# A fused attention and gated feed-forward block on one core: the four compute queues in a new order, and thirty operations on another engine

## The chip, the cores and the metric

The kernel runs on one core of a Trainium2 chip. The metric is the device time of one execution in microseconds. A core has four compute engines: TensorE (PE, matmuls; PEld are its weight loads), VectorE (DVE), ScalarE (ACT) and GpSimd (POOL). A fifth queue, SyncE (SP), issues nearly all transfers here. Each engine runs its own instructions strictly in order, and waits on semaphores for the others.

## The reference

One transformer block on x of 2048 rows by 448 columns, bf16. First a layer norm and a linear attention with 16 heads of 28:

```
qkv = layernorm(x) @ wqkv
pq = q @ w_phi ; pk = k @ w_phi                    (per head, 28x28)
phi_q = [softmax(pq), softmax(-pq)] ; phi_k likewise
kv = sum_s phi_k * v ; z = sum_s phi_k
o = (phi_q @ kv) / (phi_q @ z + 1e-6)
h = x + o @ wo
```

Then a second layer norm and a gated feed-forward with 1792 inner columns:

```
g = layernorm(h) @ w_gate ; u = layernorm(h) @ w_up
out = h + (sigmoid(g) * u) @ w_down
```

## The kernel before

The rows are cut into 16 tiles of 128, written t = 0 to 15, and into four chunks of 512 columns once they are transposed. Weights stay in SBUF. A weight or an activation has 448 inner columns, which are held as four blocks of 128 that overlap in part; matmuls use 64 rows each and run as pairs, one on the low half of the array and one on the high half. A pair of phases, named a and b (`pva4`, `pvb4`), covers one product: eight matmuls, then six. The b phase writes the banks of the a phase with the halves changed over, so it waits until the a phase has drained unless something stands between.

Every piece of work has a name, and a table `ORDER` (line 243) lists for each of the five queues the names in the order in which that engine executes them. A small graph (class `Graph`) derives the waits from what each piece reads and writes. Where a piece may run on several engines, the queue in which its name stands decides. So the order of the work, and the engine for many pieces, is written out by hand in `ORDER`, and nothing else sets it.

The names, with t a tile, c a chunk, k a block, f one of 14 blocks of inner columns of the feed-forward:

- `x`, `ld_k`, `ld_v`, `ld_q`, `ld_wo..`, `ld_wg`, `ld_wu`, `ld_wd` (SP): loads. `PACE` holds `ld_wg0` back until `pvb15` and `ld_wg1` until `kva14` have run.
- `warm` (PE, L532): matmuls on zeros, in the gaps of the head.
- `bst`, `agg` (DVE, L553, L554): row statistics of x. `pow1`, `nm1`, `nb1` (L562, L561, L569): factor, negated mean, offset. `xn` (L578 to L584): the normalised tile; on GpSimd it needs `nm1`. `xT`: its transpose, on TensorE for t below 4 (L546, copied from PSUM by `xT0e` and so on, L539), by a DMA transpose from SP for the others (L591).
- `wT`, `wTe`, `w2m0`, `w2e0`: the key weight is transposed (L607), copied, multiplied by w_phi (L620) and copied again, so that keys and their feature map are one matmul. `w2m1`, `w2e1`: the same for queries.
- `pp`, `vv` (t below 4) and `pv` (the others): feature map and values of a tile. `v1` (L539): the values copied out of PSUM. `ek` (ACT, L679, L680): the two exponentials. `ss`, `rs` (DVE, L683, L689): their sums and reciprocals. `phi` (L693): the product, on VectorE or GpSimd. `kva`, `kvb` (PE): phi times v, all tiles summed in two PSUM banks that `seed` (L717) starts.
- `pqa`, `pqb`, `eq` (L731): the queries' features, by chunk. `qs`: sums of the first two tiles. `kvzA` to `kvzD`: the finished kv, masked by heads.
- `num` (PE), then on VectorE `rsm`, `qq`, `b`, `c`, `rden` (L808 to L816) and `o` (L820): attention of a tile. `oT`: its transpose. `woa`, `wob`, `wof`: output projection; `h` (L840, L846): the residual. `sq`, `ve`, `nm`, `pow2`, `hn`, `hT`: second norm and transpose (for t of 0 and 1 `bs2` and `ag2` take the statistics from PSUM).
- `ga`, `gb` (PE, L334): gate and up of a column block f, for two tiles (names 0_f and 2_f) or a chunk of four (4_f, 8_f, 12_f). `sig` (ACT, L920): sigmoid. `uc` (ACT, L925): up copied out of PSUM, for 0_2 to 2_13. `hh` (L926): the product; on VectorE or GpSimd where `uc` exists.
- `dn`, `dp`, `dm`, `dl` (PE): down projection. `fin` (L960), `out`: last sum and store.

`num` uses PSUM banks 6 and 7 for nearly every tile, so `num6` waits until `c5` has read them. The banks of ff f are 4 and 5 for even f, 0 and 1 for odd f; a bank is free when `sig` and `uc` or `hh` have read it.

Of the kernel before, what the change touches and what calls it, by code (L numbers as in the profile page):

```python
# [18 lines left out]
class Graph:  # L19
# [109 lines left out]
    def emit(self, nc):  # L129
# [120 lines left out]
    ),  # L250
    "act": (
# [11 lines left out]
    ),  # L263
# [22 lines left out]
    ),  # L286
    "dve": (
# [15 lines left out]
    ),  # L303
    "pool": (
# [6 lines left out]
    ),  # L311
}
PACE = {"ld_wg0": "pvb15", "ld_wg1": "kva14"}
# [718 lines left out]
```

## Time and profile before

| | us |
|---|---|
| median of three runs (202.85 to 203.33) | 202.95 |
| the profiled execution | 203.83 |
| its span, first to last instruction | 202.0 |
| PE busy | 195.5 |
| DVE busy | 130.6 |
| ACT busy | 99.0 |
| POOL busy | 65.0 |

The span is the part that the profile shows in detail; the rest of the profiled execution's time lies around it. Times in the rows are microseconds from the start of the span; a row of the timeline gives the start, the length, the engine, the line, the operation and the tile, and in brackets the idle time before it and what ended it. Matmuls are pipelined, so the rows of two matmuls overlap, and the work of one is better read from start to start. The granted TensorE clock is full throughout.

### The profile page before, as it was taken

What the parts mean: (1) busy time and instruction counts of PE and PEld (TensorE: products, weight loads), DVE (VectorE), ACT (ScalarE), POOL (GpSimd) and SP (SyncE); (2) the same over time, 40 slices, a digit from 0 to 9 for tenths busy, and PEclk for the clock granted to TensorE, in tenths of its full rate; (3) what the DMA queues carried; (4) which work ended last, traced back from release to release, by engine and by line L of the source; (5) the groups of instructions that cost most, each with busy time, mean ns of one, the idle gap of its engine ahead of it and who ended that gap; (6) DMA issues with size and microseconds to landing.
All of it is one profiled execution on the core that took longest, in us unless ns stands there. A gap on an engine that the chain in (4) does not pass through costs nothing.

```text
span 202.0 us, 5879 instructions
## 1 busy us (share of the span) xinstructions
PE 195.5 (97%) x2500; PEld 114.7 (57%) x2500; DVE 130.6 (65%) x317; ACT 99.0 (49%) x212; POOL 65.0 (32%) x104
## 2 busy tenths in 40 slices
PE   7799999999989999999999999999999999999995
PEld 2745555575558887786444444555555555554443
DVE  6899999979899981646767967436432422272224
ACT  3758998798795866444333342324422212222220
POOL 5499986932425865540042020001400000000000
PEclk9999999999999999999999999999999999999999
DMA  6957542657996271221006511030212000004002
GB/s 165 303 119 126 80 83 58 178 191 242 301 190 150 55 83 27 28 55 26 5 0 81 123 29 26 3 76 23 55 49 52 2 0 3 0 3 136 0 0 91
DMA packets 32866, 16.25 MB, mean 80 GB/s; under 512 B 25096, under 2 KB 31944, under 8 KB 32840
## 3 DMA queue, kind: packets, MB, share of 16 engines
q1 hardware_dynamic: 32336, 15.86, 35.6%
q8 instruction: 19, 0.31, 0.7%
q10 hardware_dynamic: 504, 0.03, 0.2%
q14 instruction: 7, 0.06, 0.1%
HBM read 8.34 MB, written 1.84 MB: 50 GB/s over the span
## 4 chain that ended last, share of the span: by engine, by line
PE 90%; DVE 4%; DMA 2%; SPq 1%; ACT 1%; issue 1%
PE psum L334 81%; PE psum L953 5%; DMA wk_sb<-in_A_wqkv_dram 2%; DVE ss L683 2%; DVE xn_pad L581 1%; PE psum L620 1%; PE psum L532 1%; SPq L435 1%; PE psum L895 1%; PE psum L546 1%; DVE rs L689 0%; DVE b_sb L811 0%; PE psum L607 0%; DVE c_sb L814 0%; ACT v L539 0%
## 5 line engine op out<-in xcount | busy, mean ns | idle before, releaser
L334 PE MATMUL psum<-xnT,wg_sb 64*128 64x512 bf16 (+1 forms) x490 | 93.3, 334 | 0.1
L334 PE MATMUL psum<-xnT,wu_sb 64*128 64x512 bf16 (+1 forms) x490 | 92.9, 334 | 0.0
L920 ACT ACTIVATE sg_sb<-psum 128x512 bf16<-128x512 f32 (+1 forms) x70 | 35.2, 514 | 75.3 <-PE psum L334 74.8
L926 DVE TENSOR_TENSOR hhT<-sg_sb,psum 128x512 bf16<-128x512 bf16 (+1 forms) x44 | 28.9, 672 | 46.8 <-ACT sg_sb L920 46.5
L334 PEld LDWEIGHTS psum<-xnT,wg_sb 64*128 64x128 bf16 x490 | 44.4, 94 | 21.1 <-DVE hhT L926 2.3
L334 PEld LDWEIGHTS psum<-xnT,wu_sb 64*128 64x128 bf16 x490 | 44.4, 94 | 12.5
L334 PE MATMUL psum<-wd_sb,hhT 64*128 64x448 bf16 x336 | 37.1, 349 | 0.0
L334 PEld LDWEIGHTS psum<-wd_sb,hhT 64*128 64x128 bf16 x336 | 17.9, 94 | 14.0 <-DVE x_sb L846 0.5
L334 PE MATMUL psum<-Wk,xnT 64*128 64x448 bf16 x112 | 22.0, 351 | 0.1
L334 PE MATMUL psum<-wv_sb,xnT 64*128 64x448 bf16 x112 | 22.1, 351 | 0.0
L693 POOL TENSOR_TENSOR phi<-hhT,rs 128x896 bf16<-128x896 bf16 x10 | 17.7, 1775 | 2.8 <-DVE rs L689 2.6
L683 DVE TENSOR_REDUCE ss<-hhT 128x32 f32<-128x896 bf16 x16 | 16.7, 1057 | 0.2
L855 POOL TENSOR_SCALAR ve<-ssq 128x1 f32<-128x1 f32 x10 | 2.0, 202 | 45.6 <-ACT junk L852 45.3
L731 ACT ACTIVATE eq<-psum 120x1024 bf16<-120x1024 f32 x16 | 15.7, 1027 | 0.9 <-PE psum L334 0.6
L820 POOL TENSOR_TENSOR o_pad<-c_sb,rden 128x448 bf16<-128x448 bf16 x11 | 10.2, 935 | 15.7 <-DVE rden L816 13.6
L334 PE MATMUL psum<-xnT,Wq 64*120 64x512 bf16 x112 | 14.8, 384 | 0.1
L925 ACT CAST xn_pad<-psum 128x256 bf16<-128x256 f32 x26 | 9.8, 380 | 6.9 <-PE psum L334 6.4
L960 DVE SCALAR_TENSOR_TENSOR x_sb<-psum,x_sb 128x448 bf16<-128x448 f32 (+2 forms) x17 | 9.4, 592 | 3.8 <-PE psum L334 1.9
L334 PE MATMUL psum<-wo_o,oT 64*128 64x448 bf16 x49 | 11.5, 349 | 0.0
L334 PE MATMUL psum<-wo_e,oT 64*128 64x448 bf16 x49 | 11.5, 349 | 0.0
L679 ACT ACTIVATE hhT<-psum 128x448 bf16<-128x448 f32 x16 | 8.8, 547 | 5.4 <-PE psum L334 5.2
L953 PE MATMUL psum<-wd_sb,hhT 128*128 128x448 bf16 (+2 forms) x70 | 11.2, 316 | 0.0
(113 smaller groups left out, 256.9 us busy)
## 6 DMA issues: line engine op xcount, KB each, us to landing
out_dram<-x_sb SPq DMA_DIRECT2D x15, 112.0 KB, 1.8
x_sb<-in_A_x_dram SPq DMA_DIRECT2D x7, 224.0 KB, 4.9
wd_sb<-in_B_w_down_dram SPq DMA_DIRECT2D x7, 224.0 KB, 5.4
wg_sb<-in_B_w_gate_dram SPq DMA_DIRECT2D x3, 448.0 KB, 5.2
wu_sb<-in_B_w_up_dram SPq DMA_DIRECT2D x3, 448.0 KB, 4.5
wv_sb<-in_A_wqkv_dram SPq DMA_DIRECT2D x2, 224.0 KB, 5.4
wk_sb<-in_A_wqkv_dram SPq DMA_DIRECT2D x2, 196.0 KB, 3.9
wo_e<-in_A_wo_dram SPq DMA_DIRECT2D x1, 336.0 KB, 3.2
```

Of the source, the lines that this page charges most:

```text
L334: p = e.matmul(o, lhsT=w, rhs=r, start=st, stop=sp, tile_position=(row, 0))
L435: return op(eng, name, lambda e: e.dma_start(dst, src), r=r, w=w, dma="in" if eng == "sp" else "ain", nring=(48 if eng == "sp" else 8) if ...
L679: e.activation(ek[:, s, :, 0, :], src, ACT.Exp)
L683: op("dve", "ss%d" % t, lambda e: e.tensor_reduce(ss[:, s, :].rearrange("p (b h) -> p b h", h=2), eks.rearrange("p b (d h) -> p b h d", h= ...
L693: return e.tensor_tensor(phi[:, sp, :, :, :].rearrange("p b a n -> p (b a) n")[:, :, 0:56].rearrange("p b (d h) -> p b d h", h=2), eks.rea ...
L731: op("act", "eq%d_%d%s" % (c, i, "pm"[sg]), lambda e, sg=sg: e.activation(eq[c][:, sg, 2 * i:2 * i + 2, :].rearrange("p g n -> p (g n)"), ...
L820: return e.tensor_tensor(o_pad[:, t % NO, off:off + D].rearrange("p (h d) -> p h d", h=H), c_sb[:, t % NS, :, 0:DH], rden[:, t % NS, :][:, ...
L920: op("act", "sig" + nm, lambda e: e.activation(sg_sb[:, k, 0:N], bk(bg)[:, 0:N], ACT.Sigmoid), r=[B(bg)], w=[("sg", k)])
L925: op("act", "uc" + nm, lambda e: e.copy(up, bk(bu)[:, 0:N]), r=[B(bu)], w=[ub])
L926: op(("pool", "dve") if nm in UCOPY else "dve", "hh" + nm, lambda e: e.tensor_tensor(hhT[(t0 // 4) % NHH][:, ff, ns], sg_sb[:, k, 0:N], up ...
L953: p = e.matmul(bk(b)[:, lo:hi], lhsT=hb[:, ff, TS(t)], rhs=wd_sb[:, ff, lo:hi], start=ff == 0, stop=ff == FT - 1)
L960: op("dve", "fin%d%s" % (t, nm), lambda e: e.scalar_tensor_tensor(out=h_sb[:, t, lo:hi], in0=bk(b)[:, lo:hi], scalar=1.0, in1=h_sb[:, t, l ...
```

## The change

Four of the five queues of `ORDER` are rewritten; SP's stays as it is, and no operation is added or removed. The new table is one text line shorter, so the same code has line numbers lower by one afterwards.

Thirty operations change engine:

- From DVE to ACT: `xT0e`, `xT2e`, `v1_13`. From ACT to DVE: `wTe3`, `v1_11`.
- From POOL to ACT: `nm1_4`, `nm1_12`.
- From DVE to POOL: `phi8`, `hh0_2`, `hh0_5`, `hh0_6`, `hh0_9`, `hh2_1`, `hh2_2`, `hn5`, `hn6`, `ve2`, `ve6`.
- From POOL to DVE: `phi9`, `hh0_3`, `hh0_4`, `hh0_8`, `hh2_0`, `hh2_3`, `hn3`, `o9`, `nm2`, `nm3`, `nm7`, `ve5`.

Within the queues many neighbours change places. The core of the difference by queue:

```diff
 "act":
-wTe0 wTe1 xT1e wTe3 w2e0_0 w2e0_2 w2e0_3 ek0 ek1 v1_0 v1_1 ek2 w2e1_1 nm1_8 v1_2 ek3 v1_3 w2e1_3 v1_4 ek4
+wTe1 wTe0 xT1e xT0e w2e0_0 w2e0_2 w2e0_3 nm1_4 xT2e ek0 ek1 v1_0 par v1_1 ek2 w2e1_1 v1_2 v1_3 ek3 w2e1_3 nm1_8 ek4 v1_4
...
-ek6 v1_6 ek7 v1_7 v1_8 ek8 eq0_0m ek9 v1_9 ek10 v1_10 ek11 v1_11 ek12 v1_12 ek13 eq0_0p par ek14 ek15 v1_14 v1_15
+ek6 v1_6 ek7 v1_7 nm1_12 ek8 v1_8 eq0_0m ek9 v1_9 ek10 v1_10 ek11 ek12 v1_12 ek13 v1_13 eq0_0p ek14 ek15 v1_15 v1_14
...
-uc0_2 sq3 sig0_5 uc0_5 uc0_4 sig0_4 sq2 uc0_7
+uc0_2 sq2 uc0_5 sig0_5 uc0_4 sig0_4 sq3 uc0_7
...
-sig0_8 uc0_8 sq5 uc0_11 sig0_11 sig0_10 uc0_10 uc0_13 sig0_12 sig0_13 uc0_12 sq7 uc2_0 sig2_0 sig2_1 uc2_1 sq6
+uc0_8 sig0_8 uc0_11 sig0_11 uc0_10 sig0_10 sq5 sq6 sig0_13 sig0_12 uc0_13 uc0_12 sq7 uc2_0 sig2_0 sig2_1 uc2_1
 "pe":
-warm0 wT0 wT1 xT1 warm1 warm2 warm3 wT2 wT3 w2m0_0 xT0 warm4 warm5 w2m0_2 w2m0_1 w2m0_3 warm6 warm7 warm8
-ppa0 warm9 ppb0 vva0 xT2 xT3 vvb0 ppa2 ppb2 vva2 w2m1_1 vvb2 seed w2m1_0 w2m1_3 kva0 pva4 kvb0 pvb4 pva5
+warm0 wT1 wT0 warm1 xT1 warm2 warm3 xT0 w2m0_0 wT2 wT3 warm4 warm5 w2m0_2 w2m0_1 w2m0_3 warm6 warm7 warm8
+ppa0 xT2 ppb0 xT3 warm9 vva0 vvb0 ppa2 seed ppb2 vva2 w2m1_1 vvb2 kvb0 w2m1_0 w2m1_3 pva4 kva0 kvb1 pvb4 pva5
...
-pva11 kvb6 pvb11 pva12 kva6 kvb7 pvb12 kva7 kvb8 pva13 kva8 pvb13 pva14 kvb10 pvb14 pva15 kva10 kvb9 pvb15 kva9
+kvb6 pva11 kva6 pvb11 pva12 kvb7 pvb12 pva13 kva7 kvb8 pvb13 kva8 pva14 kva10 pvb14 pva15 kvb10 kva9 pvb15 kvb9
...
-kvb15 kva14 qs pqa1_1 wwo num0
+kvb15 kva14 pqa1_1 qs wwo num0
...
-ga0_10 gb0_11 gb0_10 wob6 num10 ga0_13 ga0_12 gb0_13 gb0_12 dn0_0 dn0_4 ga2_1 ga2_0
+ga0_10 gb0_11 gb0_10 num10 wob6 ga0_13 ga0_12 gb0_13 gb0_12 dn0_0 dn0_4 ga2_0 ga2_1
 "dve":
-bst2 xn0 bst3 wTe2 agg2 agg3 xT0e bst4 w2e0_1 bst5 bst7 agg4 agg5 bst6 agg7 agg6 bst11 bst8 bst10 xT2e xT3e
+xn0 bst3 bst2 agg3 wTe2 wTe3 agg2 bst5 w2e0_1 bst4 agg5 bst6 agg4 bst10 agg6 bst7 bst11 xT3e
...
-phi5 ss8 rs7 rs8 xn13 xn14 ss9 ss10 rs10 phi8 ss11 rs9 rs11 ss12 v1_13 rs12 phi11
+phi5 ss8 rs7 xn13 ss9 rs8 xn14 ss10 v1_11 rs10 ss11 rs9 rs11 ss12 phi9 rs12 phi11
...
-rsm4 qq4 bs2_1 b4 ag2_1 c4
+rsm4 bs2_1 qq4 ag2_1 b4 c4
...
-b8 hh0_2 c8 rden8 o8 ve2 hh0_5 h4 h5 rsm9 qq9 hh0_7 b9 hh0_6 nm5 c9 h6 h7 ve4
+b8 c8 hh0_4 rden8 nm3 hh0_3 o8 nm2 h4 h5 rsm9 qq9 hn3 hh0_7 b9 nm4 c9 hh0_8 ve4 rden9 h6 h7 nm5
 "pool":
-nm1_4 pow1_4 pow1_6 nm1_6 xn4 xn7 xn5 xn6 phi0 pow1_8 phi1 xn8 xn9 nb1_8 phi2 xn11 pow1_12 phi4 phi6 nm1_12
-phi7 xn15 phi10 phi9 phi12 phi13 o0 o1 o2 o3 pow2_0 pow2_1
+pow1_4 xn4 xn5 nm1_6 pow1_6 wqpad xn6 phi0 phi1 xn7 pow1_8 xn8 xn9 nb1_8 phi2 pow1_12 xn11 phi4 phi6
+phi7 phi8 xn15 phi10 phi12 phi13 o0 o1 o2 pow2_0 o3 pow2_1
...
-o6 hh0_3 hh0_4 ve3 nm2 pow2_2 hn2 pow2_3 hn3 hh0_8 hh0_11 nm6 ve5 hh0_12 pow2_4 o9 hh2_0
+o6 hh0_2 hh0_5 ve3 ve2 pow2_2 hn2 pow2_3 hh0_9 hh0_6 nm6 hh0_11 pow2_4 hh0_12 ve6
```

67 rows, old and new, of the table ORDER are left out of this document.

## The prediction

> **What bounds the kernel.** I read the page, then the table of stretches, then TensorE's waits, then the chain, and last the timeline of the places these name.
>
> ```profile
> span 202.0 us, 5879 instructions
> PE 195.5 (97%) x2500; PEld 114.7 (57%) x2500; DVE 130.6 (65%) x317; ACT 99.0 (49%) x212; POOL 65.0 (32%) x104
> ```
>
> The profiled execution took 203.83 us, 1.83 around its span; it stands 0.88 above the 202.95 us median of the runs. I sum against 203.83 and carry the difference over to the median. TensorE is busy 97%, but averages hide stages. Next the table of stretches (after the length: PE, PEld, DVE, ACT, POOL busy, then the granted clock).
>
> ```profile
> 20.00:25.00 5.00, 5.00 (x68) 2.75 (x66) 5.00 (x13) 4.79 (x12) 5.00 (x6) 1.00 0.55 80
> ```
> ```profile
> 60.00:200.00 140.00, 139.59 (x1637) 81.70 (x1628) 75.60 (x187) 52.14 (x127) 25.65 (x48) 1.00 0.21 43
> ```
>
> Two regimes. From 60 on TensorE idles 0.41 us in 140 at full clock: there a new order can lose time and hardly gain any. Before that, VectorE, and for long GpSimd, are as full as TensorE. So a gain must come from TensorE's few waits, which all lie ahead of 60:
>
> ```profile
> PE psum L532 <- DVE zero L439: 1.2, 1, 1.2
> PE psum L607 <- DMA wk_sb<-in_A_wqkv_dram: 1.0, 1, 1.0
> PE psum L334 <- DVE c_sb L814: 1.0, 1, 1.0
> PE psum L334 <- DVE phi L693: 0.7, 1, 0.7
> ```
>
> The first is the start and stays. The other three are the whole purse, 2.7 us. The chain shows where the c_sb wait ends, and that nothing but TensorE follows it for long:
>
> ```profile
> 59.03 0.55 DVE c_sb L814
> 59.58 0.14 issue
> 59.72 65.23 PE psum L334 x960
> ```
>
> **Part by part. Head (5 to 14 us).** TensorE, then ScalarE, then two VectorE rows (xn0 and wTe2):
>
> ```profile
> 7.32 0.62 PE L607 MATMUL psum<-ident,wk_sb 112*112 112x112 bf16 x8 [1.02 <-DMA wk_sb<-in_A_wqkv_dram]
> 7.77 0.36 PE L620 MATMUL psum<-Wphi,WkT 112*128 112x112 bf16 x4
> 7.97 0.39 PE L546 MATMUL psum<-ident,xn_pad 128*128 128x128 bf16 x4
> 8.19 0.67 PE L532 MATMUL psum<-zero 128*128 128x128 bf16 x9
> 8.69 0.76 PE L620 MATMUL psum<-Wphi,WkT 112*128 112x112 bf16 x12
> 9.29 1.28 PE L532 MATMUL psum<-zero 128*128 128x128 bf16 x20
> 10.50 0.93 PE L334 MATMUL psum<-Wk,xnT 64*128 64x448 bf16 x8
> ```
> ```profile
> 5.60 0.96 ACT L539 COPY WkT<-psum 112x448 bf16<-112x448 bf16 x2 [0.59 <-PE psum L607]
> ...
> 8.40 1.88 ACT L539 CAST Wk<-psum 128x448 bf16<-128x448 f32 x3
> ```
> ```profile
> 6.08 0.40 DVE L581 TENSOR_SCALAR xn_pad<-x_sb,mv,rst 128x512 bf16<-128x512 bf16 x1
> ...
> 7.76 0.39 DVE L539 COPY WkT<-psum 112x448 bf16<-112x448 bf16 x1 [0.75 <-PE psum L607]
> ```
>
> w2m0_0 and xT0 stand behind wT2 and wT3, which wait for the second wk transfer; from 7.77 to the warm matmuls at 8.19 they take 0.42. Their inputs are there by 6.56 (wTe0, wTe1) and 6.48 (xn0), so ahead of wT2 they run inside the 1.02 of idle. Everything behind then starts 0.42 earlier, if the copies keep up. wTe2 ends at 8.15, so w2m0_2 may start at about 8.27. wTe3 moves from ScalarE to VectorE, behind wTe2: 8.15 plus 0.39 gives about 8.5, in time for w2m0_3 at 8.67. ScalarE takes xT0e instead, at about 7.0 to 7.6, so its three Wk copies can follow their matmuls, the last ending near 9.9 for 10.28. The 20 warm matmuls end near 9.95, so ppa0 starts at 10.08 for 10.50. xT2 and xT3 move forward between ppa0, ppb0 and vva0, equal work in another place. nm1_4 and xT2e now stand ahead of ek0 on ScalarE: nm1_4 waits for agg4, which VectorE's queue gives at about 10.9; 0.2 and 0.6 later ek0 is due at 12.0, just in time, and ppa2, which waits for ek1's bank, keeps the 0.4. Gain 0.4; bounds 0 (ek0 0.6 late by nm1_4) and 0.5.
>
> **Middle (14 to 45 us).** VectorE loses two xT copies, phi8 and v1_13 and gains wTe3, phi9 and v1_11. The phi and v1 swaps cancel, GpSimd's too.
>
> ```profile
> L693 DVE TENSOR_TENSOR phi<-hhT,rs 128x896 bf16<-128x896 bf16 x6 | 3.8, 634 | 0.0
> ...
> L539 DVE COPY xnT<-psum 128x512 bf16<-128x512 bf16 x5 | 2.0, 419 | 0.1
> ```
>
> 2 x 0.42 less 0.39 takes 0.45 off a full VectorE; ScalarE, 4.79 of 5 full from 20 to 25, gets about that and two small nm1. The 0.7 wait, though, goes by place. It stands between kva7 and kvb8, here with phi7 and xn15 on GpSimd and a transpose's time from issue to landing:
>
> ```profile
> 34.62 0.28 PE L334 MATMUL psum<-v,phi 64*128 64x58 bf16 x8
> 35.55 0.29 PE L334 MATMUL psum<-v,phi 64*128 64x58 bf16 x8 [0.65 <-DVE phi L693]
> ```
> ```profile
> 30.75 1.74 POOL L693 TENSOR_TENSOR phi<-hhT,rs 128x896 bf16<-128x896 bf16 x1
> 32.48 0.80 POOL L584 TENSOR_SCALAR xn_pad<-x_sb,nm,rst 128x512 bf16<-128x512 bf16 x1
> ```
> ```profile
> xnT<-xn_pad SPq DMA_TRANSPOSE x12, 2.5
> ```
>
> phi8 moves to GpSimd, where it follows phi7 once rs8 is there, instead of waiting for ss9 and ss10 on VectorE; and pva13 (0.75, four steps of 0.19) stands before kva7 and kvb8 instead of behind them. If phi6, phi7 and phi8 follow each other from about 28.5 at 1.74, phi8 ends near 33.8; kvb8 is due at 34.62 - 0.4 + 0.75 + 0.1, about 35.1. The wait is gone. Late next are three with margins of a few tenths, by adding up the queues: pva13 needs v1_11, now on VectorE behind xn14 and ss10, there at about 33.8 for 34.2; pva15 needs the transpose of xn15, which moves behind phi8, so 33.9 + 0.8 + 2.5 = 37.2 for 37.4; kva10 needs phi10, behind xn15, at 36.4 for 36.6. I take 0.7 off; bounds 0 (one of them replaces it) and 0.8. xn7 moves behind phi1 on GpSimd; phi0 may start about 1.1 earlier, so xn8 still comes about 0.4 earlier, and on SP, which issues transposes in order, none becomes late. par, seed and the other kv moves cost nothing: they fill places where a second half waits for the first.
>
> **Num stage (45 to 60 us).** num6 waits for c5; VectorE's order from qq5 to hT1e is unchanged, so that 1.0 stays, and the stage starts and ends 1.1 earlier. bs2_1 ahead of qq4 swaps work. pow2_0 ahead of o3 delays o3 and so the issue of oT3 by some 0.6; it is covered by the two gate pairs ahead of woa2. pqa1_1 before qs puts qs 0.9 later, just when VectorE gets to rsm0: 0 to 0.1. The weight transfers are paced by pvb15 and kva14 and move along.
>
> **Feed-forward (60 us on).** Six hh, hn5 and hn6 go to GpSimd, five hh, hn3 and o9 come to VectorE, small ones cross both ways: about equal. Places count, and the tightest is num10, moved ahead of wob6.
>
> ```profile
> 71.11 0.28 DVE L926 TENSOR_TENSOR hhT<-sg_sb,xn_pad 128x256 bf16<-128x256 bf16 x1
> 71.31 0.64 DVE L811 TENSOR_TENSOR b_sb<-psum,qq 128x464 bf16<-128x464 f32 x1
> 71.86 0.73 DVE L926 TENSOR_TENSOR hhT<-sg_sb,xn_pad 128x256 bf16<-128x256 bf16 x1
> 72.52 0.14 DVE L850 TENSOR_SCALAR nm<-sum 128x1 f32<-128x1 f32 x1
> 72.58 0.62 DVE L814 TENSOR_TENSOR c_sb<-b_sb,psum 128x464 bf16<-128x464 bf16 x1
> 74.11 0.62 DVE L846 SCALAR_TENSOR_TENSOR x_sb<-psum,x_sb 128x448 bf16<-128x448 f32 x1 [0.91 <-PE psum L334]
> ```
>
> num10 needs c9 (ends 73.20) and would start at about 73.3: margin 0.1. An hh takes 0.28 or 0.73 here, and as many short ones (hh or hn) stand before c9 as did, so c9 moves by 0.8 earlier to 0.6 later: a stall of 0 to 0.5. wob6 then slips a num's 0.24, h6 with it, and sq6, now ahead of ScalarE's last copies of ff 12 and 13, may hold ga2_0 by 0 to 0.3. VectorE's 0.91 of idle covers the rest. I take 0, nearer the rows as they stand.
>
> Sum: -0.4 - 0.7 = -1.1. 203.83 - 1.1 = 202.7 for a profiled execution, 202.95 - 1.1 = 201.9 for the median.
>
> **Rivals.** *The two engines block each other: slower.* xn14, beside phi7 on GpSimd (30.75 to 32.49):
>
> ```profile
> 30.86 1.78 DVE L581 TENSOR_SCALAR xn_pad<-x_sb,mv,rst 128x512 bf16<-128x512 bf16 x1
> ```
>
> The shape took 0.40 for xn0 above; here it ended as phi7 did. In the new order phi6, phi7 and phi8 run without a gap while VectorE does xn13 and, one ss later, xn14; each can meet a phi just begun, 1.4 apiece. With phi9 and phi10 as a third that is up to 4.2, of which my schedule holds 0.3. v1_11's margin covers 0.4; the rest TensorE loses at pva13 and behind: at most -1.1 + 3.5, 205.3. It decides against the change from 2.1 of VectorE lateness, two long collisions, at -1.1 + 2.4 = 204.2; a typical case (two of half a phi, 1.4 in all) leaves -1.1 + 0.7, 202.5. The Trainium skill, SBUF — State Buffer, section "Who interferes with whom", has the rule: VectorE in a two-port mode, or with two SBUF inputs against a GpSimd read, and GpSimd exclude each other, and the later one fully blocks. The trace agrees: 1.78 ending with phi7. By that rule every such meeting in the new order costs the rest of the earlier instruction, which speaks against putting phi8 beside xn14.
>
> *Another wait replaces the phi wait.* xn15 or phi10 comes 0.5 to 0.8 late on a full GpSimd: the head's 0.4 remains, 202.5.
>
> *The last stage eats it.* num10 stalls 0.5 and ga2_0 0.3: 202.7.
>
> **Chances.** Forecast 0.54, its own range 201.1 to 202.3. Two long collisions 0.18 (203.6 and over); typical ones 0.08, replaced wait 0.12, last stage 0.08, these at 202.2 to 202.9. About 0.3%, 0.6 us, is what a measurement here can tell from no change. Faster: the forecast and some of the middle cases, 0.59; slower 0.20; same 0.21. The range for 8 in 10 goes from 200.9 (the c_sb wait shrinks by 1.0 as well) to 203.7.
>
> **What would show it.** Right: the wk wait shrinks from 1.0 towards 0.6, ppa0 starts near 10.1; TensorE has no phi wait; the first gate matmul, after num6, comes 1.1 earlier; from there no idle. Wrong: an xn_pad row over 1 us on VectorE around 30 to 33; a TensorE wait for v, phi or a transpose between 33 and 38, or for c_sb near 72; or a first gate matmul less than 0.5 earlier.

## The result

The changed kernel takes 202.43 us (median of 15 runs, 202.19 to 202.85) against 203.3 us before (15 runs, 202.7 to 204.73), beside each other on one chip: a ratio of 0.9964, 95% interval 0.9947 to 0.9981. That is 0.36% or 0.7 us faster, just over the 0.3% that I had set as the least a measurement tells. On another chip the same kernel gave 0.9981 (0.9965 to 0.9997). The forecast was 201.9, 0.54% faster. Its direction held, and so did the range for 8 in 10, 200.9 to 203.7; the narrow range of the forecast itself ended at 202.3, from a before of 202.95 where before now took 203.3. Its size was half as large again as the 0.36% of the first chip, and nearly three times the 0.19% of the second.

The two profiles differ by more than the timed runs: a span of 200.7 against 202.0. The changed kernel's page and its TensorE waits:

```profile
span 200.7 us, 5879 instructions
...
PE 195.7 (98%) x2500; PEld 115.2 (57%) x2500; DVE 129.1 (64%) x317; ACT 100.0 (50%) x215; POOL 64.5 (32%) x101
```
```profile
PE psum L531 <- DVE zero L438: 1.2, 1, 1.2
PE psum L333 <- DVE c_sb L813: 1.0, 1, 1.0
```

Two of the four waits are gone, the one for wk (1.0) and the one for phi (0.7); the c_sb wait of 1.0 is as it was. From the gate matmuls on, TensorE still has next to no idle (after the window come its length and the busy time of PE):

```profile
58.50:198.50 140.00, 139.78 (x1644) 81.79 (x1639) 75.23 (x189) 52.42 (x127) 25.99 (x47) 1.00 0.20 43
```

The 1.3 us can be placed by two rows of each timeline: the first product of the features, ppa0, which ends the head, and num0, which starts the num stage (ppa0 of before, at 10.50, is among the rows of the prediction).

Before:

```profile
46.53 0.40 PE L334 MATMUL psum<-kvz,eq 56*128 56x60 bf16 x16
```

After:

```profile
9.98 0.93 PE L333 MATMUL psum<-Wk,xnT 64*128 64x448 bf16 x8
...
45.19 0.41 PE L333 MATMUL psum<-kvz,eq 56*128 56x60 bf16 x16
...
58.38 65.26 PE psum L333 x960
```

Before, ppa0 began at 10.50 and num0 at 46.53, 36.03 apart; after, at 9.98 and 45.19, 35.21 apart. So the head is 0.52 shorter and the middle 0.82, and from num0 to num6 it is 13.19 both times (the last row, of the chain, starts with num6: 58.38, before 59.72). From num6 to the end of the span it is 142.3 in both. These two lengths, from the head's start to ppa0 and from ppa0 to num0, are what the experiments are read by.

### The profile page after: what moved, and what is told of

Read it like the earlier page. It is cut to its first block, busy times and chain, and to the rows that moved or that the text cites. A ratio compares the mean times of both kernels' runs of the same rounds, so it can differ in the third digit from the quotient of the medians.

```text
span 200.7 us, 5879 instructions
## 1 busy us (share of the span) xinstructions
PE 195.7 (98%) x2500; PEld 115.2 (57%) x2500; DVE 129.1 (64%) x317; ACT 100.0 (50%) x215; POOL 64.5 (32%) x101
## 4 chain that ended last, share of the span: by engine, by line
PE 97%; DVE 1%; issue 0%
PE psum L333 85%; PE psum L952 5%; PE psum L531 3%; PE psum L545 1%; PE psum L619 1%; PE psum L894 1%; PE psum L606 1%; DVE b_sb L810 0%; DVE c_sb L813 0%; PE psum L892 0%; DVE xnT L538 0%; DVE x_sb L959 0%; DVE zero L438 0%; DVE rsm L807 0%; DVE qq L808 0%
## 5 line engine op out<-in xcount | busy, mean ns | idle before, releaser
L682 DVE TENSOR_REDUCE ss<-hhT 128x32 f32<-128x896 bf16 x16 | 17.2, 1073 | 0.5 <-ACT hhT L679 0.2
L854 POOL TENSOR_SCALAR ve<-ssq 128x1 f32<-128x1 f32 x11 | 2.7, 243 | 45.9 <-ACT junk L851 45.5
L819 POOL TENSOR_TENSOR o_pad<-c_sb,rden 128x448 bf16<-128x448 bf16 x10 | 9.3, 936 | 14.0 <-DVE rden L815 13.9
L333 PEld LDWEIGHTS psum<-Wk,xnT 64*128 64x128 bf16 x112 | 7.7, 94 | 5.3 <-issue 1.3
```

Source lines behind the costliest of these rows:

```text
L333: p = e.matmul(o, lhsT=w, rhs=r, start=st, stop=sp, tile_position=(row, 0))
L682: op("dve", "ss%d" % t, lambda e: e.tensor_reduce(ss[:, s, :].rearrange("p (b h) -> p b h", h=2), eks.rearrange("p b (d h) -> p b h d", h= ...
L819: return e.tensor_tensor(o_pad[:, t % NO, off:off + D].rearrange("p (h d) -> p h d", h=H), c_sb[:, t % NS, :, 0:DH], rden[:, t % NS, :][:, ...
L854: op(("pool", "dve"), "ve%d" % t, lambda e: e.tensor_scalar(ve2[:, t:t + 1], ssq2[:, t:t + 1], 1.0 / D ** 3, EPS, op0=ALU.mult, op1=ALU.ad ...
```

## The experiments

**The kernel before, profiled again.** No edit.

> The kernel before once more, unchanged, for a second profile. Theory A (the phi wait and the wk wait are there in every execution): span 202.0 within 0.3, TensorE waits 1.0 for wk and 0.7 for phi again, and the 1.3 us between the two profiles is what the change is worth. Theory B (the first profile of before was a late one, since the timed runs differ by 0.9 us only): span 201.3 to 201.6, with a smaller phi wait because xn14 meets phi7 later or earlier on VectorE.

Its span was 201.4, not 202.0. The waits (first fence) and the two rows (second) of this second profile:

```profile
PE psum L532 <- DVE zero L439: 1.2, 1, 1.2
PE psum L334 <- DVE c_sb L814: 1.0, 1, 1.0
PE psum L334 <- DVE phi L693: 0.7, 1, 0.7
```
```profile
9.90 0.93 PE L334 MATMUL psum<-Wk,xnT 64*128 64x448 bf16 x8
...
45.93 0.41 PE L334 MATMUL psum<-kvz,eq 56*128 56x60 bf16 x16
```

The phi wait is there again, and the middle has again 36.03 us. But the wk wait is not there, and ppa0 starts at 9.90 without any change of the head: in this execution wk came earlier. Theory A was right on phi and wrong on wk and on the span; theory B was right on the span (201.3 to 201.6), and wrong in that the phi wait was no smaller.

**The head alone and the middle alone.** The new order and engines for the operations that began before 13.9 us, or for those from there to the end of the num stage. Edits, at their core:

```diff
 the head alone ("pe")
-warm3 wT2 wT3 w2m0_0 xT0 warm4
+warm3 xT0 w2m0_0 wT2 wT3 warm4
 the middle alone ("dve", "pool", "pe")
-rs7 rs8 xn13 xn14 ss9 ss10 rs10 phi8 ss11
+rs7 xn13 ss9 rs8 xn14 ss10 v1_11 rs10 ss11
-phi7 xn15 phi10 phi9
+phi7 phi8 xn15 phi10
-pvb12 kva7 kvb8 pva13
+pvb12 pva13 kva7 kvb8
```

> The kernel before with only the head (operations that began before 13.9 us) in the new order and on the new engines. Theory A: the 0.4 to 0.5 us of the head arrive at kvb8 as they are, and the phi wait grows or shrinks with them by at most 0.3, so -0.2 to -0.6 us. Rival: VectorE sets the time of phi8, so an earlier TensorE only waits longer there; VectorE too begins its sums earlier (ss0 by 1.3 us), which would make it -0.9.

> The kernel before with only the middle (13.9 to 60 us) new, head and feed-forward as before. Theory A: the phi wait goes, -0.65 to -0.85 us, no other wait takes its place. Rival: without the head's earlier start of VectorE and GpSimd the thin margins (v1_11, xn15, phi10) are missed and half of it or more stays: -0.3 or less.

The head alone: 203.83 against 203.37 us, ratio 1.0012 (0.9985 to 1.0039): nothing that shows, so both the -0.2 to -0.6 us and the rival's -0.9 missed. Its timed runs spread from 202.35 to 204.56. The middle alone: 202.25 us, 0.9949 (0.9934 to 0.9963): all of the gain, and a little more than the 0.65 to 0.85 us expected. In the head's profile TensorE waited at a new place:

```profile
6.70 0.45 PE L545 MATMUL psum<-ident,xn_pad 128*128 128x128 bf16 x4
7.64 0.36 PE L619 MATMUL psum<-Wphi,WkT 112*128 112x112 bf16 x4 [0.49 <-DMA Wphi<-in_A_w_phi_dram]
7.83 0.58 PE L606 MATMUL psum<-ident,wk_sb 112*112 112x112 bf16 x8
```

w2m0_0, moved ahead of wT2, waits for w_phi, and wT2 and wT3 stand behind it. ppa0 began at 10.56 here.

**Everything but the feed-forward.** From 60.3 us on the order and engines of before (the diff also puts back three small pieces of the head: bst8, xn5 and wqpad):

```diff
-gb0_10 num10 wob6 ga0_13
+gb0_10 wob6 num10 ga0_13
-dn0_4 ga2_0 ga2_1
+dn0_4 ga2_1 ga2_0
 (and the hh, hn, nm, ve, sq and o9 of before)
```

> The change without its feed-forward part (from 60.3 us on the order and the engines of before). Theory A: the feed-forward part costs and brings nothing, so the same as the changed kernel, ratio 0.9964 within 0.0015, and a span of 200.7. Rival: the new order there gives back a part (then this kernel is faster than the changed one by 0.2 to 0.8 us), or the old order stalls when everything comes 1.3 us earlier (then slower by 0.2 to 0.6).

202.44 us, 0.9955 (0.9941 to 0.9968), a span of 200.6. The feed-forward part costs and brings nothing that shows, as theory A had it; and beside the middle alone (0.9949, same chip, same runs of before) the head brings nothing either.

**Which move of the middle.** Three kernels, each with one move only, on the kernel before:

```diff
 phi8 to GpSimd
-rs10 phi8 ss11          ("dve")
-phi7 xn15               ("pool")
+rs10 ss11
+phi7 phi8 xn15
 pva13 forward ("pe")
-pvb12 kva7 kvb8 pva13
+pvb12 pva13 kva7 kvb8
 xn14 later ("dve")
-rs7 rs8 xn13 xn14 ss9 ss10
+rs7 xn13 ss9 rs8 xn14 ss10
```

> The kernel before with one move: phi8 from VectorE to GpSimd, behind phi7 and ahead of xn15. Theory C (in the executions of before VectorE is about 1.1 us late because xn14 waits for phi7, and everything lost in the middle comes from that): phi8 ends on GpSimd near 34.2, kvb8 does not wait, VectorE has 0.56 us less to do, so -0.5 to -0.8 us although xn14 still takes about 1.8. Rival (phi8 on GpSimd only pushes xn15 and phi10 late): -0.2 to +0.3 and a new TensorE wait near 37 to 39.

> The kernel before with one move: pva13 ahead of kva7 and kvb8 on TensorE. Theory of the prediction (pva13 alone covers the wait): -0.65 us. Theory C (VectorE stays late): the wait at kvb8 is covered, but phi14 and phi15 on VectorE are late then, so TensorE waits there, near 44, and only 0.1 to 0.3 us is left.

> The kernel before with one move on VectorE: rs7 xn13 ss9 rs8 xn14 ss10 in place of rs7 rs8 xn13 xn14 ss9 ss10, so that xn14 no longer starts just after phi7. Theory C: xn14 then waits 0.5 at most, phi8 is 0.7 to 1.1 earlier, the phi wait goes: -0.6 to -1.0 us, nearly what the whole middle brought (-1.0), and a narrower spread of the timed runs. Rival (the wait is the sum of VectorE's work, or the place of phi8): the phi wait of 0.7 stays, -0.2 to +0.2.

Measured, with the length from ppa0 to num0 from the starts of the same two rows in each profile:

| kernel | ppa0 to num0, us | against before, us | ratio of the timed runs |
|---|---|---|---|
| before, two profiles | 36.03, 36.03 | | |
| phi8 to GpSimd alone | 45.59 - 10.04 = 35.55 | -0.48 | 0.9987 (0.9966 to 1.0007) |
| pva13 forward alone | 46.16 - 10.41 = 35.75 | -0.28 | 0.9994 (0.9975 to 1.0014) |
| xn14 later alone | 44.69 - 9.48 = 35.21 | -0.82 | 0.9958 (0.9936 to 0.998) |
| the new middle alone | 45.17 - 10.07 = 35.10 | -0.93 | 0.9949 (0.9934 to 0.9963) |
| changed kernel | 45.19 - 9.98 = 35.21 | -0.82 | 0.9964 (0.9947 to 0.9981) |

The last two kernels were not timed beside the three single moves. Moving rs8 and xn14 behind ss9 on VectorE does what the whole change does. (rs8 moves along in this run, so xn14 by itself was not measured.) With xn14 moved, and everything else as before, the rows of VectorE (first) and GpSimd (second) read:

```profile
29.40 0.31 DVE L581 TENSOR_SCALAR xn_pad<-x_sb,mv,rst 128x512 bf16<-128x512 bf16 x1
29.93 1.09 DVE L683 TENSOR_REDUCE ss<-hhT 128x32 f32<-128x896 bf16 x1 [0.21 <-ACT hhT L680]
30.93 0.34 DVE L689 RECIPROCAL rs<-ss 128x32 bf16<-128x32 f32 x1
31.19 0.41 DVE L581 TENSOR_SCALAR xn_pad<-x_sb,mv,rst 128x512 bf16<-128x512 bf16 x1
```
```profile
29.76 1.68 POOL L693 TENSOR_TENSOR phi<-hhT,rs 128x896 bf16<-128x896 bf16 x1
```

xn14 takes 0.41 for 1.78, since phi7 is nearly over when it starts. phi8 stays on VectorE, and TensorE waits for no phi. pva13 alone covers the wait at kvb8, but it begins 0.19 late itself (34.72, behind v1_11 on ScalarE until 34.57), VectorE is as late as ever, and TensorE loses a part again further on, at pva15 (38.43), which needs the bank that v1_13 reads, on VectorE until 38.33. I had expected that at phi15, near 44; the place was another, the size (0.1 to 0.3 left) as expected by theory C, where the prediction's own theory, -0.65, missed. phi8 alone came out just short of its expected 0.5 to 0.8 in the profile, and in the timed runs can't be told from no change.

**xn14 back in its old place in the changed kernel.**

```diff
-phi5 ss8 rs7 xn13 ss9 rs8 xn14 ss10 v1_11
+phi5 ss8 rs7 rs8 xn13 xn14 ss9 ss10 v1_11
```

> The changed kernel with the old places of rs8 and xn14 on VectorE (rs7 rs8 xn13 xn14 ss9 ss10), everything else new. Theory C (the middle's gain is that xn14 no longer meets a phi): xn13 or xn14 waits again for phi7, 1.3 to 1.7 us; v1_11, with 0.5 of margin in the changed kernel, comes late and TensorE waits about 1 us at pva13 or soon behind, so 0.6 to 1.2 us slower than the changed kernel, near the kernel before (ratio 0.999 to 1.002). If both meet a phi, as the prediction's slower rival has it, VectorE is 3.2 late and the kernel is 2 to 2.7 us slower than the changed one (ratio 1.007 to 1.010). Rival (phi8 on GpSimd and pva13 ahead cover it): no more than 0.2 us slower, ratio 0.996 to 0.9975.

202.96 us, ratio 1.001 (0.9985 to 1.0035): the gain is gone from the timed runs, as theory C had it (0.999 to 1.002). The changed kernel with another head, timed beside it on the same chip, took 202.34 (below), 0.6 less. In the profile num0 comes 45.33 - 9.74 = 35.59 behind ppa0, 0.38 later than in the changed kernel, less than the 0.6 expected. TensorE lost it at pva13, which began at 34.26, 0.57 behind the step before it where the steps are 0.19; v1_11, behind xn14 on VectorE, ended at 34.15. xn13 and xn14, and GpSimd's three phis (phi6, phi7, phi8 in one row):

```profile
29.63 2.00 DVE L580 TENSOR_SCALAR xn_pad<-x_sb,mv,rst 128x512 bf16<-128x512 bf16 x2
```
```profile
27.82 5.36 POOL L692 TENSOR_TENSOR phi<-hhT,rs 128x896 bf16<-128x896 bf16 x3
```

Of the 2.00 xn13 took 0.31 and xn14 1.77. Only one of the two met a phi for long, so the slower rival's double collision did not come about, and its price was not measured.

**Two tries at the head.** The second wk transfer one place earlier, with the new middle and the old head; and the changed kernel with the memset bd0, which the w_phi transfers wait for, first on VectorE.

```diff
 ("sp")
-x1 x0 ld_k0 x2 ld_k2
+x1 x0 ld_k0 ld_k2 x2
 ("dve", the other kernel)
-zero steps bd0
+bd0 zero steps
```

> The new middle with the old head, and the second wk transfer issued one place earlier, ahead of x2. Theory D (the old head starts its products 3.2 us after that transfer lands, but not before about 9.9, so the head of the change brings 0 to 0.4 as the landing goes): wk lands by about 6.2, ppa0 at about 9.6 to 9.9, 0.1 to 0.4 us faster than the new middle alone (0.9949), so a ratio of 0.993 to 0.9945. Rival (the landing is not what sets the head): no difference from the new middle alone.

> The changed kernel with one memset moved: bd0, which the four w_phi transfers wait for, first on VectorE, so they are issued some 0.3 us earlier. Theory D (the head is set by the landings of wk and w_phi, which differ from one execution to the next): 0 to 0.2 us faster than the changed kernel (ratio 0.9955 to 0.9965), with fewer of the slow executions. Rival (w_phi's landing does not matter for the changed kernel): the same within 0.1.

The first took 202.96 us, 0.9973 (0.9951 to 0.9995). The new middle alone gave 0.9949 on another chip, and the two intervals overlap; but on the same chip the kernel with only xn14 moved, whose head and transfers are those of before, took 202.22. wT2 began at 5.90, so wk was early, but then TensorE stood:

```profile
5.90 0.57 PE L606 MATMUL psum<-ident,wk_sb 112*112 112x112 bf16 x8
7.49 0.36 PE L619 MATMUL psum<-Wphi,WkT 112*128 112x112 bf16 x4 [1.01 <-ACT WkT L538]
7.80 0.40 PE L545 MATMUL psum<-ident,xn_pad 128*128 128x128 bf16 x4
```

ScalarE had copied wTe1 by 6.41, so the 1.01 is not its doing. The other input of w2m0_0 is w_phi; that it came late is inferred, though the profile of the head alone showed just that. So there was no gain as theory D had it, and by its profile the head is not as before either: ppa0 began at 10.44, 0.37 behind that of the new middle alone, with 35.20 from there to num0. With bd0 first the changed kernel took 202.34 us, 0.9977 (0.9953 to 1.0002), with ppa0 at 9.71: on that chip before took 202.89, less than the 203.3 of the first, and no difference from the changed kernel can be told.

**All three moves in the head, beside the changed kernel once more.**

```diff
 ("sp")
-x1 x0 ld_k0 x2 ld_k2
+x1 x0 ld_k0 ld_k2 x2
 ("dve", over the old head)
-zero steps bd0 wopad0 wopad1 mask2 bst1 agg1 bst0 xn1 agg0 bst2 xn0 bst3
+bd0 zero steps wopad0 wopad1 mask2 bst1 agg1 bst0 xn1 agg0 xn0 bst3 bst2
```

> The new middle and the old head, with three moves in the head: the second wk transfer issued ahead of x2, bd0 first on VectorE so that w_phi is loaded some 0.3 us earlier, and bst2 behind xn0 and bst3 since x2 lands later. Theory D (wk and w_phi set the head): ppa0 at 9.3 to 9.7 instead of about 10.0, and as the middle keeps its length of 35.2 from ppa0 to num0, 0.3 to 0.7 us faster than the changed kernel. Rival: xn0, the x landings or the transposes from SP hold the middle back, and it is the same as the changed kernel within 0.2.

> The changed kernel once more, beside the kernel above. Theory: a ratio of 0.9964 within 0.0025, ppa0 between 9.7 and 10.6, and 35.2 us from ppa0 to num0 as in the first profile of it; the head differs from execution to execution, the middle does not. Rival: the middle differs too (by over 0.1).

202.55 us, 0.9978 (0.9967 to 0.999), against 202.51 us, 0.9981 (0.9965 to 0.9997): the same. ppa0 began at 10.13 in the first, so the rival holds. wT2 began at 6.37 there, but VectorE had waited for a tile of x and did wTe2, the copy of wT2, only at 7.88, and TensorE stood 0.27 for it ahead of w2m0_2: an earlier landing of wk handed the wait to the next input. The changed kernel's second profile has ppa0 at 9.73 and num0 at 44.93, 35.20 apart for 35.21: the middle repeats to 0.01 us, the head moves by 0.25. The four kernels with the new middle that are not in the table (without the feed-forward part, the two tries and the three moves) have 35.12 to 35.23. No version of the head was faster than the changed kernel by what these runs can tell.

## Why the prediction was right, and where not

- *Bounds and purse.* Right: all that was gained came from TensorE's waits ahead of 60, and from 60 on there was nothing to gain.
- *Head, -0.4.* This is the term that failed. It was priced from one execution in which wk landed late. The second wk transfer is issued at 2.60 in both kernels; in the first profile of before it landed 4.7 later, in that of the changed kernel 4.0 later (the largest value in the rows below, first before, then after). So wk was there at about 7.3 before and at about 6.6 afterwards, and this alone covers the 0.52. Where TensorE waited for wk, which is in five of the six profiles with the old head and the old transfers, ppa0 began 3.2 behind that landing; in the five profiles with the new head it began 3.3 to 3.6 behind it. The step that failed is "ahead of wT2 they run inside the 1.02 of idle": in the changed kernel xT0 began at 6.78 and w2m0_0 at 7.06, when wk had already landed, and wT2 stood behind them until 7.26. In the kernel with the head alone w2m0_0 waited for w_phi, an input that the prediction's list of inputs leaves out. The prediction's own case, a landing near 7.3 with the other inputs there, did not come about again, so whether the new head gains in it is not shown. With the old head ppa0 began at 10.50, 9.90, 10.07, 10.04, 10.41 and 9.48 in the six profiles, 10.07 on average; with the new one at 9.98, 10.56, 9.91, 9.74 and 9.73, 9.98 on average. So the head is worth 0.1 in the profiles' means, less than they scatter, and nothing in the timed runs (1.0012, and 0.9955 beside 0.9949). That the first two profiles came close to the 0.4 was luck. The lower bound of 0 was in the text, for another cause (nm1_4).

```profile
DMA to landing us min/median/max: 3.1/3.9/4.7
```
```profile
DMA to landing us min/median/max: 3.5/3.7/4.0
```

- *Middle, -0.7.* It measured -0.82, and the wait went. The reason given was half of it. I put the gain down to the places of phi8 and pva13; alone these are worth 0.48 and 0.28. What made phi8 late before was xn14's 1.78 us beside phi7, and moving rs8 and xn14 behind ss9 removes that, worth 0.82 alone; put back, the timed gain is gone. The row stood in the prediction, but as the danger of the new order, not as the cause of the old wait. So the size came out for a reason that the prediction did not give.
- *Late next.* v1_11, xn15's transpose and phi10 had margins of a few tenths by the prediction, and none of them became a wait. phi8 ended at 33.61 for 33.8 forecast, pva13 began at 34.12 for 34.2, kvb8 at 34.99 for 35.1.
- *Num stage, 0, and feed-forward, 0.* Right: 13.19 us from num0 to num6 both times, and no stall at num10, where c9 came at 71.80 for a num10 at 72.02.

```profile
71.04 0.14 DVE L849 TENSOR_SCALAR nm<-sum 128x1 f32<-128x1 f32 x1
71.16 0.64 DVE L813 TENSOR_TENSOR c_sb<-b_sb,psum 128x464 bf16<-128x464 bf16 x1
```
```profile
72.02 0.39 PE L333 MATMUL psum<-kvz,eq 56*128 56x60 bf16 x16
```

- *Rivals.* The double collision did not happen: xn14 began at 31.69 when phi7 ended at 31.72, and phi8 did not follow phi7 at once but began at 31.92 (the profile puts its last 0.20 of waiting down to TensorE; rs8, which it needs as well, ended at 31.77).

```profile
29.66 0.52 DVE L580 TENSOR_SCALAR xn_pad<-x_sb,mv,rst 128x512 bf16<-128x512 bf16 x1
30.43 1.09 DVE L682 TENSOR_REDUCE ss<-hhT 128x32 f32<-128x896 bf16 x1 [0.25 <-ACT hhT L679]
31.43 0.34 DVE L688 RECIPROCAL rs<-ss 128x32 bf16<-128x32 f32 x1
31.69 0.31 DVE L580 TENSOR_SCALAR xn_pad<-x_sb,mv,rst 128x512 bf16<-128x512 bf16 x1
```
```profile
28.06 3.66 POOL L692 TENSOR_TENSOR phi<-hhT,rs 128x896 bf16<-128x896 bf16 x2
31.92 1.69 POOL L692 TENSOR_TENSOR phi<-hhT,rs 128x896 bf16<-128x896 bf16 x1 [0.20 <-PE psum L333]
```

- *The sum.* -1.1 came from -0.4 and -0.7. The profiles say -0.52 and -0.82; with the head at its mean over the profiles it is -0.1 and -0.8, about -0.9, where the timed runs gave -0.7 (0.36%, interval 0.2 to 0.5%) and on the other chip -0.4. With the head at nothing, 0.8 is left of the 1.1, and the timed gain on the first chip is near that. The difference between the chips is left open.

Left open as well: why the timed runs of before spread more than those of the changed kernel (202.7 to 204.73 against 202.19 to 202.85 in the first comparison). The race of xn14 against phi7 could do it: with the head alone, and the old middle, xn13 and xn14 together took 0.64 in the profile, so there VectorE came first and the middle took 45.88 - 10.56 = 35.32. That before itself goes both ways was not seen: both profiles of it show the loss, and so do the three other profiles in which rs8 and xn14 have their old places, the head's apart. But the fastest timed runs of before, 201.79 to 202.11 on four later chips, are no slower than the fastest of the changed kernel on its two chips (202.19 and 202.26), which would fit executions without the loss; no profile here shows one.

```profile
30.81 0.64 DVE L580 TENSOR_SCALAR xn_pad<-x_sb,mv,rst 128x512 bf16<-128x512 bf16 x2
```
```profile
31.18 1.81 POOL L692 TENSOR_TENSOR phi<-hhT,rs 128x896 bf16<-128x896 bf16 x1
```

## What to carry to other kernels

A wait on the main engine is best followed back to the one instruction that took longer than its shape does elsewhere; here moving that one and its neighbour behind ss9 was worth as much as the whole new order. A gain that rests on the landing of a transfer needs more than one profile before it is priced, since the landing moves from one execution to the next by as much as the gain. And lengths between two fixed rows (here ppa0 to num0) show a middle part's effect where whole times scatter by half a microsecond and more: they repeated to 0.01 us in the two pairs of profiles of one kernel, and to about 0.1 us across kernels with the same middle and other heads.

## What the runs showed of the hardware

The block between VectorE and GpSimd is sharper than I had expected. A blocked xn ended about 0.15 us after the phi that it met, whatever it had waited: 32.64 for 32.49 (xn14 before), 30.18 for 30.03 (xn13 after, phi6), 31.60 for 31.44 (xn14 moved alone), 31.63 for 31.49 (xn14 moved back); free, the same instruction takes 0.31. It goes the other way too, as far as GpSimd's rows can be trusted: where xn14 came first, phi7 took 1.81 (the head alone) for 1.68 (xn14 moved alone), and in the profile before phi6, which started 0.16 behind VectorE's own phi5, took 2.07 for the 1.70 of phi4. This is what the Trainium skill, SBUF — State Buffer, section "Who interferes with whom", says: the one that starts later is blocked for the whole of the earlier instruction. And a GpSimd instruction next in its queue did not get in ahead of the VectorE instruction that already waited: in the profile before, xn15 followed phi7 on GpSimd at 32.48 and xn14 was still done at 32.64.
